# Weight conversion: two of its five operations move from ScalarE to GpSimd, and the identity matrix comes by DMA

## The chip, the core and the metric

The kernel runs on one core of one Trainium2 chip. The metric is the device time of one launch in microseconds (us); the time of a kernel is the median of its runs. Engines are named as the profile names them: PE (TensorE matmul), DVE (VectorE), ACT (ScalarE), POOL (GpSimd), SP (SyncE, which here issues most DMAs).

## The reference

Eight batches of eight heads. `phi` is turned into weights by a softmax over the sequence, the weights pool keys and values into 32 memories per head, queries attend to those memories, and the result goes through a two-layer network with the activation h cos h.

```python
a = exp(phi - max over s); a = a / (sum over s + 1e-9)
k_m = einsum('bhsm,bhsd->bhmd', a, k)
v_m = einsum('bhsm,bhsd->bhmd', a, v)
attn = softmax(q @ k_m.T / sqrt(64))          # over the 32 memories
x = (attn @ v_m) as (4608, 512)
h = x @ w_in                                  # 512 x 2048
out = (h * cos(h)) @ w_out                    # 2048 x 512
```

`w_in` and `w_out` arrive as float64. The kernel is given their bits as pairs of 32-bit words and makes float32 of them on the chip.

## The kernel before

The 4608 tokens are worked through in 12 groups of 384 (three groups for two batches of 576). A group takes 16 steps, one for each 128 columns of the hidden layer: `gemm1` makes hp (128 x 384, in PSUM), `act` and `act_end` make h cos h of it with ACT and DVE in turns, and `gemm2` adds the product with a row block of `wo` to three accumulators `acc`, four steps later (LAG). `v_m` is folded into `w_in` first, so that `gemm1` multiplies the attention weights `aT` with the folded matrix. Group 0 works in float32 (`vf`, made by `fold_first`, L454 to L460; hp at L487, acc at L538); from group 1 on all factors are split in two float16 parts (`vw`, `parts`; hp at L496, acc at L543), for which scales are needed that depend on the largest weight.

Before that, and beside the first groups, `memory(b)` and `attend(b)` prepare batch b: the maximum over the sequence (`nmx` on DVE at L222, turned by a matmul with the identity into `top`, L225), the exponential, `psA` (L250), `X`, a second product with the identity (`tpx`, L270), scores `sc`, a softmax on DVE and ACT, and the transposes into `aT`. `warm` puts matmuls that nobody reads between the parts of the start.

The weights come in 16 blocks, eight of `w_in` ("in 0" to "in 7") and eight of `w_out`, 128 x 1024 values each. `convert_next` takes one at each step of group 0 (in 0 and in 1 earlier). A block is loaded by SP into one of three raw buffers (two blocks borrow space in `wo`), and `to_float32` makes five operations of it:

- L135, DVE: the sign, from the top byte of the high word, into the upper half of the result
- L137, ACT: bits of the low word's top byte, into the lower half of the result
- L141, ACT: the high word, read as a float32, times 2^-112, in place
- L142, DVE: the high word shifted left by 3, joined with the result by a bitwise or
- L144, ACT: the squares of the result, written over the low word, with their sum into `sq`

The raw buffer is free for the next load behind L144. A block of `w_in` then goes through `fold_first` (matmuls pvf at L458, copy to `vf` at L460). When in 7 is done, `weight_scale` (L164) reduces `sq` over the partitions with `partition_all_reduce` on GpSimd (L168), and `scales` makes E, T and cu for batches 0 and 1; when the last block of `w_out` is done the same follows for `w_out`. In group 1 `w_in_split` (L187) and `w_out_split` (L178) cut the weights in two float16 parts.

GpSimd's other work before: the identity (`make_identity`: a memset and an affine select), two memsets for each batch (L273, L274), one `partition_all_reduce` for each batch (L290), and one more from batch 4 on (L213).

A scheduler decides in which order each engine's instructions stand; on an engine they start in that order. In front of an instruction of GpSimd that needs another code library than the one in place, the build puts an instruction that loads the library: library 0 holds the affine select and the tensor-scalar operation, library 1 the `partition_all_reduce`. The memsets need neither. In the lists further below such a load is a bare "ISA" that has no tile behind it.

Of the kernel before, what the change touches and what calls it, by code (L numbers as in the profile page):

```python
# [9 lines left out]

F16 = mybir.dt.float16
F32 = mybir.dt.float32
# [5 lines left out]
AF = mybir.ActivationFunctionType  # L18
ALU = mybir.AluOpType
# [4 lines left out]
P = 128  # L24
# [18 lines left out]


@with_exitstack
def attention_then_ffn(ctx: ExitStack, tc: tile.TileContext, phi, phiT, kv, qT, w_in, w_out, out):
    nc = tc.nc
    const = ctx.enter_context(tc.tile_pool(name="const", bufs=1))
    ld = ctx.enter_context(tc.tile_pool(name="ld", bufs=1))
# [7 lines left out]
        return ps_s.tile([P, 512], F32, tag="ps_s", name=name)  # L57

    ident = const.tile([P, P], F32, name="ident")
    make_identity(nc, ident)  # L60

    vmask = const.tile([P, 2, 2], F32, name="vmask")
    nc.vector.memset(vmask, 0.0)
# [62 lines left out]
    def to_float32(dst, raw, sq_to, pin=False):  # L126

        low, high = raw[:, :, :, 0], raw[:, :, :, 1]  # L130
        flat = raw.rearrange("p c f t -> p c (f t)")
        halves = dst.bitcast(I16).rearrange("p c (f t) -> p c f t", t=2)
        low_top = flat.bitcast(U8).rearrange("p c (f t) -> p c f t", t=8)[:, :, :, 3]
        high_top = flat.bitcast(I8).rearrange("p c (f t) -> p c f t", t=8)[:, :, :, 7]
        begin = (nc.vector.tensor_scalar(out=halves[:, :, :, 1], in0=high_top, scalar1=0.0, scalar2=-32768.0,  # L135
                                         op0=ALU.is_lt, op1=ALU.mult),
                 nc.scalar.activation(halves[:, :, :, 0], low_top, AF.Copy, scale=2.0 ** -5, bias=-31.0 / 64.0))  # L137
        if pin:
            for ins in begin:
                tc.keep_in_program_order(ins)  # L140
        nc.scalar.activation(high.bitcast(F32), high.bitcast(F32), AF.Copy, scale=2.0 ** -112)  # L141
        nc.vector.scalar_tensor_tensor(out=dst.bitcast(I32), in0=high, scalar=3, in1=dst.bitcast(I32),  # L142
                                       op0=ALU.logical_shift_left, op1=ALU.bitwise_or)
        nc.scalar.activation(low.bitcast(F32), dst, AF.Square, accum_out=sq_to)  # L144

    def convert_w_in(j):
        to_float32(w_in_sb[:, :, j * WS:(j + 1) * WS], loads.pop(("in", j)), sq[:, 0, j:j + 1], j == 1)

    def convert_w_out(j):
        to_float32(wo[:, 2 * j + 1:2 * j + 3], loads.pop(("out", j)), sq[:, 1, j:j + 1])  # L150
# [556 lines left out]
        gemm2(*p)  # L707


_INS = ["phi", "phiT", "kv", "qT", "w_in", "w_out"]  # L710


# [31 lines left out]
```

## Time and profile before

| what | value |
|---|---|
| median of 3 runs | 717.77 us (717.28 to 717.79) |
| span of the profiled execution, first to last instruction | 717.5 us |
| PE busy | 694.2 us (97%), 4578 instructions |
| DVE busy | 532.4 us (74%) |
| ACT busy | 526.8 us (73%) |
| POOL busy | 14.0 us (2%), 36 instructions |
| DMA | 66.70 MB, mean 93 GB/s |
| granted PE clock, mean | 0.993 |

The page gives no separate time for the profiled execution; its span of 717.5 us stands 0.27 us under the median of the runs. Rows of a timeline give the start and the duration of merged instructions in us, the engine, the line, the operation with the tiles it writes and reads, and in brackets how long the engine had been idle and what ended that. Rows of a table of windows give for each engine its busy time in a stretch, then the granted PE clock, the busy share of the 16 DMA engines, and what they moved.

### The profile page before, as it was taken

To read this page: it belongs to the slowest core of one execution; us is meant where nothing else is said; L and a number is where in the kernel's file an instruction comes from. 1 tells how busy PE (TensorE), PEld (TensorE's weight loads), DVE (VectorE), ACT (ScalarE), POOL (GpSimd) and SP (SyncE) were. 2 spreads that over 40 slices of the span, in tenths; PEclk is the share of its full clock that TensorE was granted. 3 is DMA by queue.
4 is the path that set the end of the run, shared out by engine and by line. 5 is a ranking of instruction groups with operands and counts; after the bars stand their busy time and mean duration, and the time that the engine had idled before them with its cause. 6 is when DMAs were issued, how large, how long until landed. Compare 5 with 4: busy or idle time off the path is not lost.

```text
span 717.5 us, 11780 instructions
## 1 busy us (share of the span) xinstructions
PE 694.2 (97%) x4578; PEld 357.9 (50%) x4578; DVE 532.4 (74%) x1131; ACT 526.8 (73%) x957; POOL 14.0 (2%) x36
## 2 busy tenths in 40 slices
PE   5689999999999999999999999999999999999997
PEld 2335444465554445565444544565444444555553
DVE  2678999999888795679766986579766986565552
ACT  1599999999895786778757696678767785665652
POOL 0000000000000000000000100000000000000000
PEclk9889999999999999999999999999999999999999
DMA  9985781624605300152103310152100010100101
GB/s 288 381 273 203 258 301 61 162 56 126 213 2 167 111 1 1 45 167 67 45 1 123 102 54 1 45 167 67 45 1 1 4 42 2 45 1 1 45 0 45
DMA packets 31415, 66.70 MB, mean 93 GB/s; under 512 B 2176, under 2 KB 10880, under 8 KB 31360
## 3 DMA queue, kind: packets, MB, share of 16 engines
q1 hardware_dynamic: 27040, 58.09, 25.2%
q10 hardware_dynamic: 4320, 7.87, 2.9%
q8 instruction: 36, 0.59, 0.4%
q14 instruction: 19, 0.16, 0.1%
HBM read 52.31 MB, written 9.44 MB: 86 GB/s over the span
## 4 chain that ended last, share of the span: by engine, by line
PE 82%; ACT 8%; DVE 6%; issue 2%; DMA 2%; POOL 0%; SPq 0%; POOLq 0%
PE acc L543 43%; PE hp L496 23%; PE pv L435 4%; PE psA L250 3%; PE acc L538 3%; PE hp L487 2%; PE sc L352 2%; DMA phi<-in_phi 2%; PE pv L429 1%; ACT u L518 1%; PE warm L587 1%; DVE u L513 1%; ACT raw_out L144 1%; ACT wo L137 1%; PE pvf L458 1%
## 5 line engine op out<-in xcount | busy, mean ns | idle before, releaser
L543 PE MATMUL acc<-wo,gp 128*128 128x512 f16 x1584 | 370.8, 379 | 0.0
L543 PEld LDWEIGHTS <-gp 128*128 128x128 f16 x1584 | 153.5, 98 | 162.2 <-issue 2.4
L496 PE MATMUL hp<-aT,vw 128*128 128x192 f16 (+1 forms) x1440 | 202.3, 284 | 0.7 <-DVE u L522 0.7
L518 ACT ACTIVATE u<-u,quarter 128x384 f32<-128x384 f32 x192 | 116.8, 615 | 71.0 <-DVE u L513 70.5
L496 PEld LDWEIGHTS <-vw 128*128 128x128 f16 x1440 | 125.0, 98 | 81.7 <-issue 28.2
L522 DVE SCALAR_TENSOR_TENSOR u<-hp,u 128x384 f32<-128x384 f32 x176 | 96.6, 554 | 62.5 <-ACT u L518 61.6
L513 DVE SCALAR_TENSOR_TENSOR u<-hp,cu,gp 128x192 f32<-128x192 f32 (+1 forms) x240 | 114.7, 503 | 24.2 <-ACT gp L508 22.9
L508 ACT ACTIVATE gp<-hp,cu 128x192 int32<-128x192 f32 (+1 forms) x240 | 111.3, 492 | 19.7 <-PE hp L496 13.5
L525 DVE TENSOR_TENSOR gp<-u,gp 128x384 f16<-128x384 f32 x176 | 96.4, 552 | 34.8 <-ACT gp L524 34.1
L524 ACT CAST gp<-u 128x384 f16<-128x384 f32 x176 | 88.3, 508 | 44.2 <-DVE u L522 43.9
L538 PE MATMUL acc<-wo,gp 128*128 128x512 f32 x96 | 44.8, 597 | 0.0
L442 DVE SCALAR_TENSOR_TENSOR vw<-pv,vw 128x512 f16<-128x512 f32 x48 | 33.0, 689 | 6.8 <-ACT vw L441 6.3
L441 ACT ACTIVATE vw<-pv 128x512 f16<-128x512 f32 x48 | 28.4, 592 | 7.3 <-PE pv L435 6.8
L487 PE MATMUL hp<-aT,vf 128*128 128x384 f32 x64 | 26.7, 550 | 5.4 <-DVE gp L520 2.1
L559 ACT ACTIVATE ob<-acc,os 128x512 f32<-128x512 f32 x28 | 18.5, 683 | 14.6 <-PE acc L543 12.7
L518 ACT ACT_TABLE_LOAD x20 | 25.7, 1283 | 0.4
L538 PEld LDWEIGHTS acc<-wo,gp 128*128 128x128 f32 x96 | 17.3, 190 | 16.9 <-issue 14.7
L250 PE MATMUL psA<-kv,phi 128*32 128x129 f32 (+1 forms) x640 | 23.7, 280 | 0.0
L487 PEld LDWEIGHTS hp<-aT,vf 128*128 128x128 f32 x64 | 12.3, 207 | 18.7 <-issue 6.9
L250 PEld LDWEIGHTS psA<-kv,phi 128*32 128x32 f32 (+1 forms) x640 | 16.4, 110 | 10.4 <-issue 7.6
L352 PE MATMUL sc<-q,km 128*64 128x256 f32 (+3 forms) x192 | 20.0, 335 | 0.1
L352 PEld LDWEIGHTS sc<-q,km 128*64 128x64 f32 x192 | 11.4, 138 | 10.7 <-issue 5.7
(130 smaller groups left out, 545.3 us busy)
## 6 DMA issues: line engine op xcount, KB each, us to landing
kv<-in_kv SPq DMA_DIRECT2D x32, 516.0 KB, 6.0
q<-in_qT SPq DMA_DIRECT2D x8, 1152.0 KB, 5.7
raw_out<-in_w_out SPq DMA_DIRECT2D x8, 1024.0 KB, 5.3
out<-ob ACTq DMA_DIRECT2D x30, 256.0 KB, 2.3
raw_in<-in_w_in SPq DMA_DIRECT2D x6, 1024.0 KB, 7.9
phi<-in_phi SPq DMA_DIRECT2D x8, 512.0 KB, 5.4
w_in_sb<-w_in_parts SPq DMA_DIRECT2D x12, 256.0 KB, 4.1
phiT<-in_phiT SPq DMA_DIRECT2D x4, 576.0 KB, 7.4
```

The source lines that it names most:

```text
L250: nc.tensor.matmul(psA[32 * j:32 * (j + 1), g * KV:(g + 1) * KV], lhsT=a[:n, c, h * M:(h + 1) * M], rhs=kvs[c][:n, h * KV:(h + 1) * KV], s ...
L352: nc.tensor.matmul(sc[D * p:D * (p + 1), g * n:(g + 1) * n], lhsT=km[:, 2 * g + p], rhs=qt[:, 2 * g + p, t0:t0 + n], start=True, stop=True)
L487: nc.tensor.matmul(hp[:, :GT], lhsT=st["vf", q][:, g, fo * P:(fo + 1) * P], rhs=st["aTf"][:, g], start=(g == 0), stop=(g == 1))
L496: nc.tensor.matmul(hp[:, c0:c0 + n], lhsT=vw[:, wi, g, fo * P:(fo + 1) * P], rhs=aT[:, ai, g, c1:c1 + n], start=(k == 0), stop=(k == 5))
L508: ins = nc.scalar.activation(ni[:, c0:c0 + n], hp[:, c0:c0 + n], AF.Copy, scale=turns, bias=0.25)
L513: nc.vector.scalar_tensor_tensor(out=u[:, c0:c0 + n], in0=hp[:, c0:c0 + n], scalar=turns, in1=ni[:, c0:c0 + n], op0=ALU.mult, op1=ALU.subt ...
L518: nc.scalar.activation(u, u, AF.Sin, scale=TWO_PI_BELOW, bias=quarter)
L522: nc.vector.scalar_tensor_tensor(out=u, in0=hp[:, :GT], scalar=2.0 ** -17, in1=u, op0=ALU.mult, op1=ALU.mult)
L524: nc.scalar.copy(gp[:, 0], u)
L525: nc.vector.tensor_tensor(out=gp[:, 1], in0=u, in1=gp[:, 0], op=ALU.subtract)
L538: nc.tensor.matmul(accs[grp][t], lhsT=gp[:, t * P:(t + 1) * P], rhs=wo[:, f + 1], start=(f == 0), stop=(f == NF - 1))
L543: nc.tensor.matmul(accs[grp][t], lhsT=gp[:, gi, t * P:(t + 1) * P], rhs=parts[:, wi], start=(f == 0 and gi == 0 and wi == 0), stop=(f == N ...
```

## The change

In `to_float32` the two operations of L137 and L141 are made by `nc.gpsimd.tensor_scalar` and no longer by `nc.scalar.activation`. The identity is no longer made on GpSimd: the host hands in `np.eye(128)` and SP loads it, ahead of every other load.

```diff
-    make_identity(nc, ident)
+    nc.sync.dma_start(out=ident, in_=eye)
...
                  nc.vector.tensor_scalar(out=halves[:, :, :, 1], in0=high_top, scalar1=0.0, scalar2=-32768.0,
                                          op0=ALU.is_lt, op1=ALU.mult),
-                 nc.scalar.activation(halves[:, :, :, 0], low_top, AF.Copy, scale=2.0 ** -5, bias=-31.0 / 64.0))
+                 nc.gpsimd.tensor_scalar(out=halves[:, :, :, 0], in0=low_top, scalar1=2.0 ** -5, scalar2=-31.0 / 64.0,
+                                         op0=ALU.mult, op1=ALU.add))
         if pin:
             for ins in begin:
                 tc.keep_in_program_order(ins)
-        nc.scalar.activation(high.bitcast(F32), high.bitcast(F32), AF.Copy, scale=2.0 ** -112)
+        nc.gpsimd.tensor_scalar(out=high.bitcast(F32), in0=high.bitcast(F32), scalar1=2.0 ** -112, scalar2=1.0,
+                                op0=ALU.mult, op1=ALU.mult)
...
-_INS = ["phi", "phiT", "kv", "qT", "w_in", "w_out"]
+_INS = ["phi", "phiT", "kv", "qT", "w_in", "w_out", "eye"]
...
+        "eye": np.eye(P, dtype=np.float32),
```

In the changed kernel's lists the lines are numbered a little differently: L134 is the sign, L136 and L141 are the two operations on GpSimd, L143 is the shift-and-or, L145 the squares; the all-reduces stand at L169 and L291.

GpSimd before, from the all-reduce of batch 0 (l_0) to the one for `w_out` (m_out). One library load stands here, the one for the all-reduces (the other, for the affine select, stands further up); `km` and `vm` are the memsets of a batch.

```order
L290 ISA
L290 ISA l_0_228<-l_0_226 128x1
L273 MEMSET km_481 128x256
L290 ISA l_1_520<-l_1_518 128x1
L273 MEMSET km_1615 128x256
L274 MEMSET vm_1616 128x256
L168 ISA m_in<-m_in 128x1
L168 ISA m_out<-m_out 128x1
```

GpSimd now, around the all-reduce of batch 1 (l_1): raw_out_297 and raw_out_304 are the blocks out 1 and out 2, raw_in_308 and raw_in_324 the blocks in 4 and in 5.

```order
L136 TENSOR_SCALAR wo<-raw_out_297 128x1024
L141 TENSOR_SCALAR raw_out_297<-raw_out_297 128x1024
L136 TENSOR_SCALAR wo<-raw_out_304 128x1024
L141 TENSOR_SCALAR raw_out_304<-raw_out_304 128x1024
L291 ISA
L291 ISA l_1_517<-l_1_515 128x1
L136 ISA
L136 TENSOR_SCALAR w_in_sb<-raw_in_308 128x4x256
L141 TENSOR_SCALAR raw_in_308<-raw_in_308 128x1024
L136 TENSOR_SCALAR w_in_sb<-raw_in_324 128x4x256
L141 TENSOR_SCALAR raw_in_324<-raw_in_324 128x1024
```

GpSimd now, around the two all-reduces for the weights' scales: raw_out_537, raw_out_576 and raw_out_602 are out 5, out 6 and out 7, raw_in_491 is in 7.

```order
L141 TENSOR_SCALAR raw_in_491<-raw_in_491 128x1024
L141 TENSOR_SCALAR raw_out_537<-raw_out_537 128x1024
L169 ISA
L169 ISA m_in<-m_in 128x1
L136 ISA
L136 TENSOR_SCALAR wo<-raw_out_576 128x1024
L141 TENSOR_SCALAR raw_out_576<-raw_out_576 128x1024
L136 TENSOR_SCALAR wo<-raw_out_602 128x1024
L141 TENSOR_SCALAR raw_out_602<-raw_out_602 128x1024
L275 MEMSET vm_1613 128x256
L169 ISA
L169 ISA m_out<-m_out 128x1
```

What moved on GpSimd: 32 tensor-scalar operations now stand between the all-reduces, and each change from the one kind to the other has a library load in front of it. The whole list has seven loads where there were two: one ahead of l_0, one behind it, one on each side of l_1, one on each side of m_in, one ahead of m_out; none follows later.

DVE before, from the end of batch 1's sums (l_1) to the conversion of in 5: the conversions stand among the steps of group 0.

```order
L288 TENSOR_REDUCE l_1_518<-l_1_515 128x1
L513 SCALAR_TENSOR_TENSOR u_6_551<-hp_6_548,gp_6_552 128x384
L154 TENSOR_SCALAR ev_522<-l_1_520 128x1
L155 TENSOR_SCALAR ev_522<-ev_522 128x1
L135 TENSOR_SCALAR w_in_sb<-raw_in_311 128x4x256
L520 TENSOR_TENSOR gp_6_552<-hp_6_548,u_6_551 128x384
L142 SCALAR_TENSOR_TENSOR w_in_sb<-raw_in_311,w_in_sb 128x4x256
L135 TENSOR_SCALAR w_in_sb<-raw_in_327 128x4x256
L513 SCALAR_TENSOR_TENSOR u_7_584<-hp_7_581,gp_7_585 128x384
L460 COPY vf_496<-pvf_497 128x2x256
L354 STREAM_TRANSPOSE at_526<-sc_0_529 128x512
L142 SCALAR_TENSOR_TENSOR w_in_sb<-raw_in_327,w_in_sb 128x4x256
```

DVE now at the same place; the softmax of batch 1 (at_523) stands behind the last row here.

```order
L155 TENSOR_SCALAR ev_519<-l_1_517 128x1
L156 TENSOR_SCALAR ev_519<-ev_519 128x1
L134 TENSOR_SCALAR w_in_sb<-raw_in_324 128x4x256
L134 TENSOR_SCALAR wo<-raw_out_373 128x1024
L223 TENSOR_REDUCE nmx_1426<-phiT_604 128x2
L143 SCALAR_TENSOR_TENSOR w_in_sb<-raw_in_308,w_in_sb 128x4x256
L143 SCALAR_TENSOR_TENSOR w_in_sb<-raw_in_324,w_in_sb 128x4x256
L143 SCALAR_TENSOR_TENSOR wo<-raw_out_373,wo 128x1024
L355 STREAM_TRANSPOSE at_523<-sc_0_526 128x512
L359 TENSOR_REDUCE rm_524<-at_523 128x16
L360 TENSOR_TENSOR at_523<-at_523,rm_524 128x512
```

What moved on DVE: the shift-and-or of three blocks (in 4, in 5, out 3) now stand in a row, ahead of the whole softmax of batch 1 and of the steps of group 0 from the eighth on; before, the softmax's first rows and a step stood between them.

More of the change, by code (lines that the diff above doesn't have):

```diff
@@ L7 @@
 from concourse import bass_isa, mybir
-from concourse.masks import make_identity
 from concourse._compat import with_exitstack
@@ L45, in attention_then_ffn @@
 @with_exitstack
-def attention_then_ffn(ctx: ExitStack, tc: tile.TileContext, phi, phiT, kv, qT, w_in, w_out, out):
+def attention_then_ffn(ctx: ExitStack, tc: tile.TileContext, phi, phiT, kv, qT, w_in, w_out, eye, out):
     nc = tc.nc
```

## The prediction

> **What bounds the kernel now.** I read the table of windows first: where does PE, the engine with 97% of the span, still wait? Columns: stretch, length, busy time of PE, PE weight loads, DVE, ACT and POOL, granted clock, DMA share, GB/s.
>
> ```profile
> 0.00:24.00 24.00, 16.64 (x122) 7.47 (x122) 5.77 (x22) 3.57 (x7) 1.85 (x10) 1.00 0.94 315
> 24.00:50.00 26.00, 16.50 (x68) 8.13 (x68) 19.82 (x31) 22.44 (x30) 0.31 (x1) 0.80 0.91 312
> 50.00:100.00 50.00, 48.75 (x249) 24.16 (x248) 45.04 (x86) 48.81 (x70) 1.33 (x4) 1.00 0.73 249
> 100.00:130.00 30.00, 30.00 (x127) 14.13 (x126) 28.64 (x67) 29.99 (x54) 0.78 (x1) 1.00 0.46 145
> 130.00:717.00 587.00, 582.29 (x4016) 303.97 (x4014) 433.13 (x928) 421.99 (x801) 9.75 (x20) 1.00 0.18 58
> ```
>
> From 100 us on PE has no slack: 4.7 us idle in the last 587. Whatever is lost or won by 130 us stays in the total, one for one. From 50 to 130 ACT is full (48.81 of 50, 29.99 of 30), and the conversions are a good part of that; but PE waits only 1.25 us there. So a full ACT costs next to nothing now. What PE waits for stands in its timeline:
>
> ```profile
> 11.81 1.22 PE L225 MATMUL top<-ident,nmx 128*128 128x128 f32 x4 [5.57 <-POOL ident masks.py:199]
> ```
>
> ```profile
> 33.90 4.76 PE L487 MATMUL hp<-aT,vf 128*128 128x384 f32 x8 [1.88 <-DVE aT L375]
> ...
> 40.37 1.56 PE L487 MATMUL hp<-aT,vf 128*128 128x384 f32 x4 [0.69 <-ACT vf L460]
> 44.00 2.31 PE L487 MATMUL hp<-aT,vf 128*128 128x384 f32 x4 [2.08 <-DVE gp L520]
> ...
> 71.51 1.08 PE L458 MATMUL pvf<-w_in_sb,vm 128*64 128x256 f32 x8 [0.50 <-DVE w_in_sb L142]
> ...
> 90.79 0.91 PE L487 MATMUL hp<-aT,vf 128*128 128x384 f32 x2 [0.74 <-ACT vf L460]
> ```
>
> The first wait is for the identity. Behind the first hp, the waits that ACT's load could be blamed for sum to 0.69 + 2.08 + 0.50 + 0.74 = 4.0 us: the most that taking work off ACT can win. Last, the timeline of POOL, for the engine that gets the work:
>
> ```profile
> 0.73 0.20 POOL masks.py:197 MEMSET ident<- 128x128 f32 x1 [0.29 <-POOLq L732]
> 0.87 0.32 POOL L273 MEMSET km<- 128x256 f32 x1
> 11.47 0.28 POOL masks.py:199 TENSOR_SCALAR_AFFINE_SELECT ident<-ident 128x128 f32<-128x128 f32 x1 [10.28 <-issue]
> 11.72 0.55 POOL L274 MEMSET vm<- 128x256 f32 x2
> 23.11 0.38 POOL L290 PARTITION_ALL_REDUCE l<-l  x1 [10.84 <-DVE l L288]
> ```
>
> POOL stood still for 10.28 us ahead of the affine select, with nothing to wait for but the library load that the lists show there. This is the price on which the forecast rests; the second load hides in the 10.84 us wait for DVE.
>
> **The identity by DMA.** `top` no longer waits for POOL. Its other input is done at 4.57 + 1.35 + 0.45 = 6.4 us (first row below, plus one DMA issue that now stands ahead on SP, as long as that of phiT, 0.44), and the first ten warm matmuls end about there too. So the start moves up by 11.8 - 6.4 = 5.4 us, if the loads keep up; the nearest limit is q, issued at 5.06 and landed by 5.06 + 12.8 + 0.45 = 18.3, while the scores would want it at 24.13 - 5.4 = 18.7.
>
> ```profile
> 4.57 1.35 DVE L222 TENSOR_REDUCE nmx<-phiT 128x2 f32<-128x1152 f32 x1 [2.84 <-DMA phiT<-in_phiT]
> ```
>
> ```profile
> 24.13 1.52 PE L352 MATMUL sc<-q,km 128*64 128x256 f32 x16
> ```
>
> ```profile
> 5.06 0.63 SPq L100 DMA_DIRECT2D q<-in_qT  x1
> ```
>
> ```profile
> DMA to landing us min/median/max: 5.6/9.2/12.8
> ```
>
> **One conversion on POOL.** ACT loses 16 times (1.36 + 1.14) = 40 us, at the durations of these rows:
>
> ```profile
> L137 ACT ACTIVATE w_in_sb<-raw_in x6: 1337/1360/1392, 23.8 to 90.6; 128x1024 int16<-128x1024 uint8 x6
> L135 DVE TENSOR_SCALAR w_in_sb<-raw_in x6: 704/729/766, 27.2 to 92.4; 128x1024 int16<-128x1024 int8 x6
> L141 ACT ACTIVATE raw_in<-raw_in x6: 1111/1137/1179, 28.0 to 94.2; 128x1024 f32<-128x1024 f32 x6
> L142 DVE SCALAR_TENSOR_TENSOR w_in_sb<-raw_in,w_in_sb x6: 1182/1224/1227, 29.1 to 95.4; 128x1024 int32<-128x1024 int32 x6
> ```
>
> What POOL needs for 1024 columns no row shows. From below, its memsets: 0.20 us for 128 columns, 0.32 for 256, so 0.08 + 8 x 0.12 = 1.04. From above, eight affine selects of 128 columns at 0.28: 2.26. I take 0.1 fixed and the rest of the affine select, which reads as well as writes, eight times: 0.1 + 8 x 0.18 = 1.55 us, 3.1 for a block.
>
> **A library load.** The one row says 10.28 us, at a DMA share of 0.94. If all of it is transfer and goes with that share, it is 10.28 x 0.73 / 0.94 = 8.0 in the window from 50 to 100 and 10.28 x 0.46 / 0.94 = 5.0 from 100 to 130; if none of it is, 10.28 everywhere. I take the middles, 9.1 and 7.7, with 5.0 and 10.28 as ends. [...] No row here shows a load beside quiet DMA queues.
>
> **The sum, load by load.** Ahead of the first block stand l_0 (23.11 + 0.38 - 5.4 = 18.1) and a load at full DMA share, 10.3: 28.4. The block takes 3.1, DVE's or 1.22, pvf and the copy to `vf` 1.6: first hp at 34.3 against 33.90. The 5.4 us are gone. Of the waits at 40 and 44 (2.8 us) I give half back, for an ACT that is free; the sign of out 1 (row below) then starts at 55.7.
>
> ```profile
> 56.68 0.75 DVE L135 TENSOR_SCALAR wo<-raw_out 128x1024 int16<-128x1024 int8 x1
> ...
> 70.14 1.23 DVE L142 SCALAR_TENSOR_TENSOR w_in_sb<-raw_in,w_in_sb 128x1024 int32<-128x1024 int32 x1 [1.56 <-ACT raw_in L141]
> ...
> 73.50 0.72 DVE L354 STREAM_TRANSPOSE at<-sc 128x512 f32<-128x512 f32 x1 [0.17 <-PE sc L352]
> ...
> 86.05 0.56 DVE L520 TENSOR_TENSOR gp<-hp,u 128x384 f32<-128x384 f32 x1
> ...
> 95.36 1.23 DVE L142 SCALAR_TENSOR_TENSOR w_in_sb<-raw_in,w_in_sb 128x1024 int32<-128x1024 int32 x1 [0.34 <-ACT raw_in L141]
> ```
>
> Out 1 and out 2 keep POOL until 55.7 + 2 x 0.75 + 3 x 1.55 = 61.9 (the other 1.55 lies beside DVE). Load 9.1, l_1 0.38, load 9.1: 80.4. In 4 is through POOL at 83.5, through DVE at 84.7, against 71.4 in the trace: +13.3. PE has work of its own until about 73, then it waits: this is the first large stall. On DVE the rows that follow now stand behind out 3, which is through at 83.5 + 4 x 1.55 + 1.2 = 90.9; from there to the end of step 8 (gp) stand 19 rows, of which the 73.50 and the 86.05 row are two of a kind with the first and the last, that sum to 12.0 us in the trace: 102.9 against 86.6, +16.3. In 7, five rows on, moves alike, from 95.4 to 111.7.
>
> The scales. Out 5 leaves POOL at 111.7 + 2.5 (three DVE rows) + 1.55 = 115.8; load 7.7, m_in 0.4, some 14 operations of 0.15 on DVE (2.1), then the first `parts` and three to four `vw` on ACT and DVE (4.3, at 0.7 each): 130.3. The first hp of group 1 stood at 112.13: +18.2.
>
> ```profile
> 112.13 0.34 PE L496 MATMUL hp<-aT,vw 128*128 128x192 f16 x2
> ...
> 129.83 0.81 PE L543 MATMUL acc<-wo,gp 128*128 128x512 f16 x3
> ```
>
> From m_in at 123.9 a load (7.7), out 6 and out 7 (6.2), a load (7.7), m_out 0.8, its eight small operations with larger ones between (3.0) and the first `w_out_split` (1.5) lead to 150.8 for the first acc of group 1, which stood at 129.83: +21.0. PE's own work from 130.3 would have had it there at 148.0, so this load still costs 2.8. Behind it nothing is left to hide in: 717.5 + 21.0, with the 0.27 us by which the median lies over the profiled span, is 738.8. With loads of 5.0 and POOL operations of 1.04 the same sum gives +3.6, 721; with loads of 10.28, +31, 749. A stalled PE would also lose clock (0.80 in the window from 24 to 50, where it idles a third of the time), some 2 us that I leave to the upper end.
>
> **The rivals.** (1) Short loads, faster. If a load beside lighter DMA costs no more than ACT's own table load (row below, 1.28 us), the 5.4 us of the start stay and POOL keeps up: 717.8 - 5.4 with a little of the 4.0 is 711.8. It decides at in 4: the two loads there cost 18.2 and the delay is 13.3, so at 2.5 us each the sign turns. The 10.28 us row speaks against it; for it, only that that row lies in the busiest DMA window.
>
> ```profile
> 41.44 1.28 ACT L518 ACT_TABLE_LOAD   x1
> ```
>
> (2) POOL and DVE hold each other up. In the new order the sign and the or on DVE (0.73 and 1.22) lie beside POOL's operations of the next block. If one waits for the other's whole instruction, each of the 9 blocks from in 4 on loses up to 1.55 us, 14 in all, half of it where DVE waits anyway: 738.8 + 7 to 14, 746 to 753. No row of before has a reading POOL beside DVE. [...] (3) POOL's operation is as slow as its upper bound: 14 on the path by 0.7 more, +10, 749. (4) All of it hides, since conversions are made ahead: within 1.4 us of before. Against it: DVE's list puts three ors in front of the softmax, so a late block holds more than itself.
>
> **Chances.** Loads that stall the path, 721 to 749: 0.72. (2) 0.12, (3) 0.05, (1) 0.08, (4) 0.03. A measurement of this kernel can tell about 0.2%, 1.4 us. Slower by more: 0.89; within: 0.03; faster: 0.08. The range leaves out (1), (4) and the top of (2) and (3): 721 to 752.
>
> **What would show it.** In the changed kernel: `top` at about 6.4; POOL idle "issue" of 5 to 10 us in front of the first L136, l_1, the L136 behind it, and m_in; POOL operations near 1.55; pvf of in 4 waiting some 12 us for DVE; the first acc of group 1 near 151 and PE full behind it. Loads under 3 us, or an acc at 125, would make it wrong; DVE operations beside POOL that take longer than their rows here would show (2).

## The result and the profile after

The changed kernel takes 739.81 us (median of 4 runs, 738.66 to 741.28) against 717.77 before: 1.0301 times, with an interval of 1.0284 to 1.0318. The forecast was 738.8, within 721 to 752. All medians here are over undisturbed runs: one of experiment 9 (2510 us, the profiled one, so its trace isn't used) and one of before beside it (810.88 us) are left out.

The table of windows of the changed kernel, with the columns as before: PE, PE weight loads, DVE, ACT, POOL, granted clock, DMA share, GB/s.

```profile
24.00:50.00 26.00, 15.24 (x56) 7.93 (x57) 22.22 (x27) 11.64 (x20) 16.68 (x12) 0.67 0.97 337
50.00:100.00 50.00, 35.99 (x192) 18.39 (x191) 31.15 (x54) 21.28 (x36) 17.93 (x13) 0.83 0.58 198
100.00:130.00 30.00, 28.51 (x87) 12.31 (x85) 26.82 (x57) 17.86 (x32) 9.58 (x8) 1.00 0.54 179
130.00:160.00 30.00, 28.63 (x150) 14.63 (x149) 26.38 (x58) 24.45 (x49) 6.96 (x6) 1.00 0.28 72
```

Most of the loss stands in the second row: PE works 36.0 of the 50 us where it worked 48.75 before, at a clock of 0.83 instead of 1.00, while ACT, which was relieved, works only 21.3 and DVE 31.2. All compute engines wait there. The page's first part gives the account of the whole span: PE busy 698.5 us instead of 694.2, at a span of 739.1 instead of 717.5. So 4.3 us are slower matmuls, and the other 17.3 of the 21.6 us are waits.

The waits stand in PE's timeline (start, duration, what it does, and in brackets the idle time and what ended it):

```profile
7.03 0.71 PE L226 MATMUL top<-ident,nmx 128*128 128x128 f32 x4 [1.25 <-DVE nmx L223]
...
13.79 0.65 PE L251 MATMUL psA<-kv,phi 128*32 128x129 f32 x16 [1.38 <-DMA kv<-in_kv]
...
32.27 1.98 PE L459 MATMUL pvf<-w_in_sb,vm 128*64 128x256 f32 x8 [10.54 <-DVE w_in_sb L143]
34.92 1.65 PE L488 MATMUL hp<-aT,vf 128*128 128x384 f32 x2 [0.67 <-ACT vf L461]
...
86.02 1.98 PE L459 MATMUL pvf<-w_in_sb,vm 128*64 128x256 f32 x8 [10.77 <-DVE w_in_sb L143]
...
130.34 0.73 PE L497 MATMUL hp<-aT,vw 128*128 128x192 f16 x5
...
150.14 0.38 PE L544 MATMUL acc<-wo,gp 128*128 128x512 f16 x1
151.13 1.89 PE L544 MATMUL acc<-wo,gp 128*128 128x512 f16 x8 [0.61 <-DVE wo L182]
```

`top` starts 4.8 us earlier than before, the first hp 1.0 later. Then in 4 makes PE wait 10.77 us at 86.02, the first hp of group 1 comes at 130.34 instead of 112.13, and the first `acc` of group 1 at 150.14 instead of 129.83: 20.3 of the 21.6 us, with one more wait of 0.61 us right behind it. Behind the waits stands POOL:

```profile
17.46 0.35 POOL L291 PARTITION_ALL_REDUCE l<-l  x1 [15.93 <-DVE l L289]
25.25 1.33 POOL L136 TENSOR_SCALAR w_in_sb<-raw_in 128x1024 int16<-128x1024 uint8 x1 [7.43 <-issue]
26.66 1.09 POOL L141 TENSOR_SCALAR raw_in<-raw_in 128x1024 f32<-128x1024 f32 x1
...
70.94 0.38 POOL L291 PARTITION_ALL_REDUCE l<-l  x1 [6.76 <-issue]
82.12 1.32 POOL L136 TENSOR_SCALAR w_in_sb<-raw_in 128x1024 int16<-128x1024 uint8 x1 [10.80 <-issue]
83.52 1.09 POOL L141 TENSOR_SCALAR raw_in<-raw_in 128x1024 f32<-128x1024 f32 x1
84.69 2.40 POOL L136 TENSOR_SCALAR w_in_sb<-raw_in 128x1024 int16<-128x1024 uint8 x1
...
124.96 0.38 POOL L169 PARTITION_ALL_REDUCE m_in<-m_in  x1 [8.10 <-issue]
132.71 1.36 POOL L136 TENSOR_SCALAR wo<-raw_out 128x1024 int16<-128x1024 uint8 x1 [7.37 <-issue]
...
145.22 0.68 POOL L169 PARTITION_ALL_REDUCE m_out<-m_out  x1 [6.00 <-issue]
```

Each switch between a conversion and an all-reduce has an idle time that nothing but "issue" ended: 7.43, 6.76, 10.80, 8.10, 7.37 and 6.00 us, 46.5 in all. These are the library loads of the list. The bare operations are short, 1.33 and 1.09 us, but L136 at 84.69, beside the shift-and-or of DVE, takes 2.40.

### The profile page after: what moved, and what is told of

It reads as the page before. It is cut to its first block, busy times and chain, and to the rows that moved or that the text cites. A ratio compares the mean times of both kernels' runs of the same rounds, so it can differ in the third digit from the quotient of the medians.

```text
span 739.1 us, 11813 instructions
## 1 busy us (share of the span) xinstructions
PE 698.5 (95%) x4578; PEld 360.1 (49%) x4578; DVE 541.6 (73%) x1130; ACT 494.8 (67%) x926; POOL 62.2 (8%) x66
## 4 chain that ended last, share of the span: by engine, by line
PE 73%; DVE 12%; DMA 5%; ACT 5%; POOL 3%; issue 2%; SPq 1%; POOLq 0%
PE acc L544 41%; PE hp L497 21%; PE pv L436 3%; DMA kv<-in_kv 2%; PE psA L251 2%; PE sc L353 2%; DMA phi<-in_phi 2%; DVE u L514 1%; PE hp L488 1%; DVE w_in_sb L143 1%; POOL wo L136 1%; DVE wo L143 1%; ACT u L519 1%; POOL raw_out L141 1%; DVE at L370 1%
## 5 line engine op out<-in xcount | busy, mean ns | idle before, releaser
L459 PE MATMUL pvf<-w_in_sb,vm 128*64 128x256 f32 x64 | 12.2, 517 | 24.9 <-DVE w_in_sb L143 23.1
L291 POOL PARTITION_ALL_REDUCE l<-l x8 | 3.0, 380 | 340.7 <-DVE l L289 334.0
L145 ACT ACTIVATE raw_in<-w_in_sb 128x1024 f32<-128x1024 f32 x6 | 7.0, 1163 | 31.6 <-DVE w_in_sb L143 27.0
L353 PE MATMUL sc<-q,km 128*64 128x256 f32 (+3 forms) x192 | 21.8, 360 | 1.1 <-issue 0.6
```

Of the source, the lines that this page charges most:

```text
L353: nc.tensor.matmul(sc[D * p:D * (p + 1), g * n:(g + 1) * n], lhsT=km[:, 2 * g + p], rhs=qt[:, 2 * g + p, t0:t0 + n], start=True, stop=True)
```

## The experiments

Before was run again beside each experiment, with medians of 718.41 us beside experiments 1 to 4, 718.42 beside 5 to 8, 718.71 beside 9 and 10, and 717.78 beside 11. What a kernel costs is given as its excess over these; the changed kernel's own is 22.0. Brackets behind a ratio hold its 95% interval.

**1. The identity by DMA alone.**

```diff
 (before)
-    make_identity(nc, ident)
+    nc.sync.dma_start(out=ident, in_=eye)
```

> The kernel before with only the identity's part of the change: SP loads it, both conversions stay on ACT. Theory (library loads that stand ahead of conversions made the change slow, and the identity by itself gains the wait for the first load): top starts near 7.0 us as in the changed kernel, the start is about 5 us earlier and that stays, since ACT takes the first block when it has landed (about 21 us): 712 to 714 us. Rival (the start is bound by the transfers of kv, q and the first block, so the identity was never worth anything): 716 to 718 us.

718.9 us, 0.9996 [0.9979, 1.0013]: no change, and the expected gain is missed. But the start did move, against the rival. That shows in this run's timelines, PE's and then ACT's with the squares of in 4 and in 7 and the loads of function tables (ACT_TABLE_LOAD) between them:

```profile
30.07 5.46 PE L486 MATMUL hp<-aT,vf 128*128 128x384 f32 x8 [1.43 <-DVE aT L374]
...
93.13 2.44 PE L486 MATMUL hp<-aT,vf 128*128 128x384 f32 x4 [2.41 <-DVE gp L519]
...
112.19 1.17 PE L495 MATMUL hp<-aT,vw 128*128 128x192 f16 x12
```

```profile
68.60 1.14 ACT L143 ACTIVATE raw_in<-w_in_sb 128x1024 f32<-128x1024 f32 x1
...
74.69 1.28 ACT L407 ACT_TABLE_LOAD   x1
...
78.95 1.28 ACT L517 ACT_TABLE_LOAD   x1
...
80.88 1.28 ACT L407 ACT_TABLE_LOAD   x1
...
90.57 1.28 ACT L517 ACT_TABLE_LOAD   x1
...
96.73 1.15 ACT L143 ACTIVATE raw_in<-w_in_sb 128x1024 f32<-128x1024 f32 x1
```

ACT's timeline of before, for the same two blocks:

```profile
71.59 1.18 ACT L144 ACTIVATE raw_in<-w_in_sb 128x1024 f32<-128x1024 f32 x1
...
78.17 1.28 ACT L408 ACT_TABLE_LOAD   x1
...
84.11 1.28 ACT L518 ACT_TABLE_LOAD   x1
...
97.17 1.23 ACT L144 ACTIVATE raw_in<-w_in_sb 128x1024 f32<-128x1024 f32 x1
```

The first hp is 3.8 us ahead of before (33.90), the squares of in 4 still 3.0, those of in 7 only 0.4, and group 1 starts where it did. In the window from 50 to 100 ACT is busy 49.55 of 50 us here and 48.81 before. So the lead is given back while ACT has hardly a gap. Between the two blocks ACT needs 2.6 us more than before, and the rows say for what: four table loads instead of two, 2 x 1.28 us, since the new order takes the softmax's exponentials (L407) in two pieces with a step's activation (L517) between them. Two ACT instructions more, and most of PE's lead is gone: that points to ACT as what binds before in this stretch, although PE hardly waits there, and to the scheduler's order as what took most of the lead. Experiment 7 below starts nearly as early and has two table loads there; it keeps 1.7 us of its lead at in 7 (squares at 95.43) and 1.0 at the first `acc` of group 1 (128.82). Where the rest of the lead went was not taken apart.

**2. The conversion alone**: the changed kernel, with the identity made on GpSimd again.

```diff
 (after)
-    nc.sync.dma_start(out=ident, in_=eye)
+    make_identity(nc, ident)
```

> The changed kernel with the identity made on GpSimd again, so that only the conversion's part of the change is left; eight library loads and the affine select ahead. Theory: the start is 5 to 6 us later than in the changed kernel, everything that waits for GpSimd moves with it: 743 to 747 us. Rival (the stage is paced by DVE's list from 50 us on, and the start hides in it): 739 to 741 us.

743.88 us, 1.0352 [1.0328, 1.0375], excess 25.5, as expected. Beside the conversion the identity's DMA is worth 3.4 us, alone nothing: here GpSimd's early work is on the path, the first conversion starts at 29.83 instead of 25.25.

**3. All early maxima on PE**: l_0, l_1, m_in and m_out are taken by a matmul with the identity and a DVE reduction, so that no load stands between conversions.

```diff
 (after)
+    def all_max(dst, src, name):
+        t = small_ps(name)[:, 0:P]
+        nc.tensor.matmul(t, lhsT=src.broadcast_to([P, P]), rhs=ident, start=True, stop=True)
+        nc.vector.tensor_reduce(out=dst, in_=t, op=ALU.max, axis=AX.X)
...
-        nc.gpsimd.partition_all_reduce(m, m, channels=P, reduce_op=RED.max)
+        all_max(m, m, f"am_{name}")
...
-        nc.gpsimd.partition_all_reduce(l3, l2, channels=P, reduce_op=RED.max)
+        if b < 2:
+            all_max(l3, l2, f"al_{b}")
+        else:
+            nc.gpsimd.partition_all_reduce(l3, l2, channels=P, reduce_op=RED.max)
```

> The changed kernel, but the maximum over the partitions for l_0, l_1, m_in and m_out is made by a matmul with the identity and a reduction on DVE instead of partition_all_reduce, so that no library load stands between conversions (one ahead of the first, one behind the last). All 32 operations stay on GpSimd, beside the same DVE operations. Theory: the stalls at the first block, at in 4 and ahead of the scales go; the two scale maxima now hold PE for some 1 to 3 us each: 709 to 717 us. Rival (GpSimd and DVE hold each other up, or GpSimd's operations are too slow): it keeps most of the loss, 728 us or more.

723.22 us, 1.0067 [1.0042, 1.0093]. Neither the theory nor the rival: without loads between conversions 17.2 of the 22.0 us are gone, but it does not get ahead of before. PE's wait for in 4 shrinks from 10.77 to 1.80 us (PE's timeline):

```profile
72.07 1.08 PE L467 MATMUL pvf<-w_in_sb,vm 128*64 128x256 f32 x8 [1.80 <-DVE w_in_sb L143]
```

What is left shows in DVE's timeline:

```profile
85.59 1.23 DVE L143 SCALAR_TENSOR_TENSOR wo<-raw_out,wo 128x1024 int32<-128x1024 int32 x1
86.73 1.32 DVE L373 TENSOR_SCALAR rs<-rs 128x16 f32<-128x16 f32 x1
...
91.32 1.33 DVE L378 TENSOR_TENSOR at<-at,rs 128x640 f32<-128x640 f32 x1
...
102.31 2.10 DVE L143 SCALAR_TENSOR_TENSOR wo<-raw_out,wo 128x1024 int32<-128x1024 int32 x1
```

An operation on 16 columns takes 1.32 us (the same line on 20 columns 0.16), the 640 columns 1.33 (0.81 in experiment 7), the or 2.10 instead of 1.23. POOL's timeline has conversions beside all three (at 85.63, 90.84 and 102.05): DVE seems to wait inside its operations.

**4. The loads alone**: experiment 1 plus a one-column operation on GpSimd behind each conversion, whose result nobody reads.

```diff
 (experiment 1)
+    tiny = const.tile([P, 1], F32, name="tiny")
...
         nc.scalar.activation(low.bitcast(F32), dst, AF.Square, accum_out=sq_to)
+        nc.gpsimd.tensor_scalar(out=tiny, in0=dst[:, 0, 0:1], scalar1=1.0, scalar2=1.0, op0=ALU.mult, op1=ALU.mult)
```

> The first kernel of this call (identity by DMA, conversions on ACT) with one GpSimd operation on a single column behind each conversion, whose result nobody reads: the same changes of library between the all-reduces, without the long operations. Theory: the loads take 6 to 11 us here too, but no conversion waits for them, only m_in and m_out are late, by 6 to 8 us, of which some is hidden: 2 to 8 us above the kernel with the identity alone. Rival (the loss comes from the long operations beside DVE): within 1 us of the kernel with the identity alone. If loads by themselves cost 15 us or more, waiting conversions aren't the point.

720.64 us, 1.0024 [1.0013, 1.0035]: 1.7 us over experiment 1, just short of the theory's 2 to 8 and above the rival's 1. The loads are there, as POOL's timeline shows:

```profile
25.28 0.20 POOL L145 TENSOR_SCALAR tiny<-w_in_sb 128x1 f32<-128x1 f32 x1 [7.55 <-DVE w_in_sb L142]
...
107.94 0.38 POOL L169 PARTITION_ALL_REDUCE m_in<-m_in  x1 [9.43 <-issue]
115.09 0.34 POOL L145 TENSOR_SCALAR tiny<-wo 128x1 f32<-128x1 f32 x1 [6.78 <-ACT vw L442]
121.43 0.44 POOL L169 PARTITION_ALL_REDUCE m_out<-m_out  x1 [6.00 <-DVE u L514]
129.22 0.54 POOL L145 TENSOR_SCALAR tiny<-wo 128x1 f32<-128x1 f32 x1 [7.35 <-issue]
```

m_in comes 8.5 us later than in experiment 1 (99.47), m_out 9.1 later (112.33), yet the first hp of group 1 loses 2.2 us (114.40) and its first acc 0.5 (130.32 against 129.80). All its loads together cost 1.7 us while no conversion is queued behind them; by themselves they do not make the 22.0.

**5. and 6. The maxima of one kind on PE**: in 5 those of the weights' scales (m_in, m_out), in 6 those of the softmax over the sequence (l_0, l_1). Each is one half of the edit of experiment 3.

```diff
 (after; 5)
-        nc.gpsimd.partition_all_reduce(m, m, channels=P, reduce_op=RED.max)
+        all_max(m, m, f"am_{name}")
 (after; 6)
-        nc.gpsimd.partition_all_reduce(l3, l2, channels=P, reduce_op=RED.max)
+        if b < 2:
+            all_max(l3, l2, f"al_{b}")
+        else:
+            nc.gpsimd.partition_all_reduce(l3, l2, channels=P, reduce_op=RED.max)
```

> The changed kernel with the maxima of m_in and m_out taken by a matmul with the identity and a DVE reduction, as in the run with all four maxima on PE; l_0 and l_1 stay on GpSimd, so the loads around them stay and those around the two scales go. The loads were worth 16.6 us together. My theory: they act in two places that both count. Up to in 7 all is as in the changed kernel (pvf of in 4 waits some 11 us, or of in 7 at 113); then 7 us in front of m_in go, the first hp of group 1 stands near 123 instead of 130, and the first acc of group 1 follows PE's own 17.7 us later near 141 instead of 151: 728 to 732. Rival: the stall at in 4 carries nearly all, and the loads at the scales lie beside PE work: 735 to 740, the first acc at 148 or later. Second rival: the scales carry nearly all: 722 to 726.

> The mirror of the run before: l_0 and l_1 by a matmul and DVE, m_in and m_out stay on GpSimd with the loads ahead of and behind each. My theory: up to in 7 as in the run with all maxima on PE (in 4 waits under 2 us, out 5 ready near 101), then a load of 6 to 8 us ahead of m_in: first hp of group 1 near 121 (113.5 without loads), first acc of group 1 near 141 (133.3 without, 151 with all loads): 728 to 732, so that both halves sum to the 16.6 us. Rival (in 4's stall carries nearly all): 722 to 726. Second rival (the scales carry all): 736 to 740.

5: 734.48 us, 1.0234 [1.0207, 1.0261]; 6: 729.69 us, 1.0146 [1.0120, 1.0173]. The second lies where my theory had it, the first 2.5 us above, short of the rival. Against the changed kernel's 22.0 the excess falls by 6.0 (to 16.1) and by 10.8 (to 11.3), together 16.8, where both at once gave 17.2: two separate places that add up, with some two thirds at l_0 and l_1. POOL's timelines, of 5 and then of 6, have the loads that are left:

```profile
80.47 1.33 POOL L136 TENSOR_SCALAR w_in_sb<-raw_in 128x1024 int16<-128x1024 uint8 x1 [11.15 <-issue]
```

```profile
113.95 0.38 POOL L174 PARTITION_ALL_REDUCE m_in<-m_in  x1 [9.87 <-issue]
121.32 1.34 POOL L136 TENSOR_SCALAR wo<-raw_out 128x1024 int16<-128x1024 uint8 x1 [6.99 <-issue]
...
134.00 0.86 POOL L174 PARTITION_ALL_REDUCE m_out<-m_out  x1 [5.89 <-DVE u L531]
```

In 6, with the same loads at the scales as in experiment 4, m_in comes 6.0 us later than there and m_out 12.6 later (134.00 against 121.43): between the two, out 6 and out 7 now go through POOL as well.

**7. Identity by DMA and maxima on PE, conversions on ScalarE.**

```diff
 (experiment 1)
-        nc.gpsimd.partition_all_reduce(m, m, channels=P, reduce_op=RED.max)
+        all_max(m, m, f"am_{name}")
...
-        nc.gpsimd.partition_all_reduce(l3, l2, channels=P, reduce_op=RED.max)
+        if b < 2:
+            all_max(l3, l2, f"al_{b}")
+        else:
+            nc.gpsimd.partition_all_reduce(l3, l2, channels=P, reduce_op=RED.max)
```

> The identity by DMA and the four maxima on PE, conversions on ScalarE as in the kernel before: GpSimd does no reduction early and no conversion. It shows what the substitute for the maxima costs by itself. My theory: nothing that counts, so 717 to 720, equal to the run with the identity alone (718.9), and the 4.3 us by which the run with GpSimd conversions and maxima on PE lies above that are the conversion's own. Rival: the matmuls by the identity and their PSUM buffer hold up the path, 721 to 724; then GpSimd's conversion without loads costs about nothing.

717.21 us, 0.9984 [0.9971, 0.9997], as my theory had it. It is the fastest of all, but its interval ends at 0.9997, too near to 1 to be counted as a gain. The substitute for the maxima costs nothing that shows, so the conversion on GpSimd without any load costs 723.22 - 717.21 = 6.0 us.

**8. to 11. Parts of the conversion on GpSimd, without loads**: 8 has only the high word's scaling there, 9 and 11 (the same kernel twice) only the low word's bits, 10 both operations for the eight blocks of `w_out` alone.

```diff
 (experiment 3; 8)
-                 nc.gpsimd.tensor_scalar(out=halves[:, :, :, 0], in0=low_top, scalar1=2.0 ** -5, scalar2=-31.0 / 64.0,
-                                         op0=ALU.mult, op1=ALU.add))
+                 nc.scalar.activation(halves[:, :, :, 0], low_top, AF.Copy, scale=2.0 ** -5, bias=-31.0 / 64.0))
 (experiment 3; 9 and 11)
-        nc.gpsimd.tensor_scalar(out=high.bitcast(F32), in0=high.bitcast(F32), scalar1=2.0 ** -112, scalar2=1.0,
-                                op0=ALU.mult, op1=ALU.mult)
+        nc.scalar.activation(high.bitcast(F32), high.bitcast(F32), AF.Copy, scale=2.0 ** -112)
 (experiment 3; 10, and the same for the high word)
+                 nc.gpsimd.tensor_scalar(...) if pool else nc.scalar.activation(...)
...
+        to_float32(wo[:, 2 * j + 1:2 * j + 3], loads.pop(("out", j)), sq[:, 1, j:j + 1], pool=True)
```

> The run with all maxima on PE, and the low word's bits made by ScalarE again: GpSimd does only the high word's scaling (one operation of 1.10 us a block, no load between). My theory: the 4 to 5 us that were left there come from GpSimd's 2.40 us operations beside DVE's or and the or's own lengthening; with half of them gone, 716.5 to 720, the or back at 1.22 us in most blocks. Rival: they come from the length of the chain over three engines and DVE's order, which stays: 722 to 724.

> All maxima on PE, the high word's scaling on ScalarE again, the low word's bits on GpSimd: the mirror of the run before, so no load between conversions. Without loads both operations cost 6.0 us over the run with the conversions on ScalarE (723.2 against 717.2), the high word's alone 2.4, while DVE's busy time summed over 716 us went from 533.5 to 543.0 with both and to 536.2 with the high word's alone: nearly the same steps. My theory: the price is DVE time, lost where DVE and GpSimd hold each other up, and the low word's operation, which in the list stands beside the or of the block ahead, carries the rest: 720 to 722, with DVE's sum near 540. Rival: the price is one handover more in a block's chain, the same for either operation: 719 to 720, DVE's sum unrelated.

> All maxima on PE, and both operations on GpSimd for the eight blocks of w_out alone; the eight of w_in are converted with ScalarE. No pvf of group 0 waits for a block of w_out. Theory (DVE time lost by the two engines holding each other up, wherever the block lies): half the price, 719.5 to 721.5, DVE's sum near 538. Rival (the longer chain of a block is what costs, where pvf waits for it): nothing is left, 716.5 to 718, whatever DVE's sum does.

> The same kernel as the run with the low word's bits alone on GpSimd, whose profiled execution was disturbed (2510 us) and shows no DVE sum. Theory (DVE time lost by mutual holding up): 720 to 722 again, DVE's busy time near 540 in 716 us, DVE's or lengthened. Rival (one handover, the same for either operation): 719 to 720, DVE's sum near 536 or below.

The table of windows ends with sums over the first 716 us, here of experiments 7, 8, 10, 11 and 3, in this order:

```profile
sum 716.00, PE 695.13 PEld 358.33 DVE 533.45 ACT 528.12 POOL 12.02; mean PE 115.86 PEld 59.72 DVE 88.91 ACT 88.02 POOL 2.00
```

```profile
sum 716.00, PE 696.22 PEld 359.33 DVE 536.18 ACT 513.22 POOL 31.02; mean PE 116.04 PEld 59.89 DVE 89.36 ACT 85.54 POOL 5.17
```

```profile
sum 716.00, PE 696.93 PEld 359.47 DVE 536.36 ACT 513.20 POOL 34.46; mean PE 116.16 PEld 59.91 DVE 89.39 ACT 85.53 POOL 5.74
```

```profile
sum 716.00, PE 692.12 PEld 357.21 DVE 540.31 ACT 511.06 POOL 33.77; mean PE 115.35 PEld 59.54 DVE 90.05 ACT 85.18 POOL 5.63
```

```profile
sum 716.00, PE 692.69 PEld 358.31 DVE 542.95 ACT 493.97 POOL 63.22; mean PE 115.45 PEld 59.72 DVE 90.49 ACT 82.33 POOL 10.54
```

| experiment | on GpSimd | us | excess | DVE busy |
|---|---|---|---|---|
| 7 | nothing | 717.21 | -1.2 | 533.5 |
| 8 | high word | 719.61 | +1.2 | 536.2 |
| 10 | both, `w_out` only | 720.25 | +1.5 | 536.4 |
| 11 (9) | low word | 720.60 (720.53) | +2.8 (+1.8) | 540.3 |
| 3 | both | 723.22 | +4.8 | 543.0 |

Against before the ratios are 1.0014 [1.0002, 1.0026] (8), 1.0028 [1.0009, 1.0047] (9), 1.0025 [1.0012, 1.0038] (10) and 1.0036 [1.0020, 1.0052] (11). DVE has 1132 to 1134 instructions in each of the five by the page, and its time rises by up to 9.5 us while ACT loses 34: the more GpSimd does, the longer DVE takes, and the time follows. In 10 no pvf waits for a block that goes through GpSimd, and about half of the 6.0 us is still paid; so the longer chain of a block of `w_in` is not the whole price. The steps between 8 and 11 are about as large as the intervals. That the price is DVE's lengthening fits all five; that nothing else has a part in it is not shown.

## Why the prediction was right, step by step

**Start.** `top` at 6.4 predicted, 7.03 measured; l_0 done at 18.1 predicted, at 17.81 measured (17.46 + 0.35). The limit named (q) was the wrong transfer: psA waited 1.38 us for kv.

**First block.** Two errors cancelled. The load beside a busy DMA (share 1.04 in that stretch, first row of the table below) was put at 10.3 and took 7.43; but the or stood behind softmax operations of DVE that had become 1.01 and 1.76 us long, and took 2.29 itself. First hp 34.3 predicted, 34.92 measured.

**POOL's operation.** 1.55 us was mis-sized in both directions: 1.32 and 1.09 alone (at 82.12 and 83.52, while DVE is idle), up to 2.40 beside DVE. Over the 16 blocks L136 sums to 30.0 us and L141 to 18.8 (the groups by line), so a block takes 3.05 against 3.1 predicted. The mean was right for the wrong reason.

**The stall at in 4.** Predicted through DVE at 84.7, measured 85.88 (84.65 + 1.23); pvf was to wait some 12 us and waited 10.77. Loads of 9.1 each were predicted, 6.76 and 10.80 came: 17.6 instead of 18.2. The rows by load, of the changed kernel, show that the model behind the middle values is false (the column before the last is the DMA share):

```profile
18.00:25.00 7.00, 3.73 (x27) 2.32 (x25) 4.22 (x9) 0.64 (x3) 0.00 (x0) 0.94 1.04 394
64.20:70.90 6.70, 6.70 (x18) 3.15 (x17) 4.76 (x10) 2.99 (x6) 0.00 (x0) 1.00 0.84 279
71.40:82.10 10.70, 3.85 (x9) 1.34 (x8) 2.96 (x5) 0.00 (x0) 0.00 (x0) 0.91 0.69 250
...
125.40:132.70 7.30, 6.29 (x34) 3.04 (x33) 6.83 (x24) 5.59 (x10) 0.00 (x0) 1.00 0.00 0
139.30:145.20 5.90, 5.90 (x23) 2.94 (x22) 5.90 (x12) 4.92 (x10) 0.00 (x0) 1.00 0.00 0
```

The longest load ran at a share of 0.69, loads at 1.04 and 0.84 were shorter, and with no other DMA traffic at all two took 7.37 and 6.00. So 6 to 7.4 us are not transfer of other queues' making, and what is above that doesn't go with the share.

**The scales.** Loads of 7.7 predicted, 8.10, 7.37 and 6.00 measured; first hp of group 1 predicted and measured at 130.3; first acc 150.8 predicted, 150.14 measured, with the next at 151.13.

**Clock.** The 2 us left to the upper end were 4.3 us of longer matmuls, with 0.67 and 0.83 granted in the two stalled windows. They lie inside the stretch up to 150 us.

**The sum as a whole.** With the loads as they came (7.43; 6.76 and 10.80; 8.10, 7.37 and 6.00) and 3.05 us for a block, the prediction's own steps lead to +15.4 for the first acc, 733.2 us, which is 6.6 below the measured time. The loads were put too long, and two things that the sum had at nothing did come: DVE's operations lengthened beside GpSimd's, and matmuls were longer by 4.3 us. How the 6.6 us divide between them is not shown. So the path and the stalls are right, but that 738.8 lies within 1.0 us of 739.81 is in good part luck. The other end says the same: short loads were to give 711.8, and experiment 3, without a load between conversions, took 723.22. The lower end of the range is not what its steps give either: with loads of 5.0 behind the first and operations of 1.04 they lead to +1.1, 719, and not to +3.6.

**What before is bound by.** Here the prediction read the profile wrongly, without harm to the number: "a full ACT costs next to nothing now". Its 4.0 us count only the waits that stand in the trace, and not a lead that a full ACT takes back. Experiment 1 puts a lead of 3.8 us in front of a full ACT, and all but 0.4 is gone at in 7, with 2.6 us of table loads more in ACT's list.

**The rivals.** Short loads (1): the loads were 6.0 or more, and even with none (experiment 3) the kernel is slower than before. POOL and DVE holding each other up (2) does happen: GpSimd's L136 took 2.40 us beside the or, against 1.32 with DVE idle, and beside GpSimd's operations the or took 2.10 instead of 1.23 us and an operation on 16 columns 1.32 instead of the 0.16 of before. What makes the two engines hold each other up no run here shows. Without loads the conversion on GpSimd costs 6.0 us, and the holding up is the likely cause of it; how much it adds beside the loads is not shown. The POOL operation as slow as its upper bound (3) did not come, with a mean of 1.5 us, nor did full cover (4).

## What to carry to other kernels

An engine that is 2% busy (14.0 us of POOL before) isn't free: ask what its instructions need in place before they start, and how often they alternate with instructions that need something else. A switch kept GpSimd idle for 6 to 11 us here, which was nearly harmless (1.7 us for all of them in experiment 4) until work that others wait for was queued behind it (without the loads between conversions 17.2 of the 22.0 us went, in experiment 3). And where an engine is full over a long stretch, that PE barely waits in it doesn't mean that it binds nothing: give PE a lead ahead of that stretch and see whether it survives (of 3.8 us in experiment 1 0.4 was left at in 7). And compare the full engine's list before and after: a new order of the same work can hold more table loads (four instead of two between in 4 and in 7 in experiment 1, 1.28 us each).

## What was not expected of the hardware

- A library load between GpSimd's tensor-scalar operation and its `partition_all_reduce` kept GpSimd idle for 5.9 us (5.86, ahead of m_out in experiment 2) to 11.2 (11.15, ahead of in 4 in experiment 5) where "issue" ended the wait, and six of the seven switches of the changed kernel show such a wait. There the two loads at a DMA share of 0.00 took 6.00 (to the all-reduce) and 7.37 (to the tensor-scalar operation), the longest, 10.80, ran at a share of 0.69, and the one of 7.43 at 1.04: the share doesn't tell the length.
- Beside GpSimd's 1024-column operations DVE's small operations lengthen too: a tensor-scalar operation on 16 or 24 columns takes 0.16 to 0.18 us in before and up to 1.32 (experiment 3), the or 1.22 in before and up to 2.31 (changed kernel). GpSimd's own L136 takes 1.32 with DVE idle (changed kernel, at 82.12) and up to 2.45 (experiment 5).
